# Talking-heads attention and expert layers: two sets' mixes and two score units in one stretch of 64x64 tiles every fourth step, copies out of PSUM dealt to ScalarE and VectorE

## The chip, the core and the metric

The kernel runs on one core of one Trainium2 chip. The metric is the device time of one execution in microseconds (us); three executions of the kernel before took 1455.02, 1460.07 and 1455.32 us, median 1455.32. The engines are TensorE (PE in the profile, with its weight loads as PEld), VectorE (DVE), ScalarE (ACT), GpSimd (POOL) and SyncE (SP), whose queue issues the DMA transfers. Each engine works through its own list of instructions in order.

## The reference

Eight batches, 12 heads, 448 positions, 64 values per head. Scores are mixed over the heads before the softmax (w_pre) and the softmax's result is mixed over the heads after it (w_post); then come the values, and three matrix layers on the 3584 tokens:

```python
scores = scale * np.matmul(q, k.transpose(0, 1, 3, 2))
scores = np.einsum('bhij,hg->bgij', scores, w_pre)
scores = scores - np.max(scores, axis=-1, keepdims=True)
attn = np.exp(scores)
attn = attn / (np.sum(attn, axis=-1, keepdims=True) + 1e-09)
attn = np.einsum('bhij,hg->bgij', attn, w_post)
x = np.matmul(attn, v)
a = x @ w1
b = x @ w2
out = (a * b @ w3) @ w_out
```

## The kernel before

**Attention.** A *score unit* (`qk`, line 173) makes the scores of a pair of heads for 128 rows of queries, four matmuls in 64x64 tiles into two PSUM banks; two copies (lines 178 and 179) bring them to SBUF as `st`, and SyncE stores them to DRAM as `raw`. They are read back as `r` by *sets*: a set is 2 x 10 query rows with all 12 heads, so that heads lie along the partitions. There are 180 sets. For each set `mix` (line 219) multiplies by w_pre (four matmuls in 64x64 tiles into `psm`), `largest` (line 226, VectorE) finds the row minimum of the negated scores (`mn`), `exp` (line 234, ScalarE) makes `e` and its sums `sm`, and `scale` makes the reciprocal `ri` (lines 243 and 244, VectorE) and from it the scaled w_post, `w` (line 246, GpSimd; `w2` in the code). `post` (line 259) multiplies `e` by it: 28 small matmuls in 64x64 tiles into `pso`, which `put` (line 273) copies to `mt` on ScalarE. When `mt` holds 150 columns (15 units of 10), `av` (line 300) multiplies it by the values: 24 matmuls for half of the heads, in 128x64 tiles, into `psa`.

**Background.** Between these, TensorE makes *background matmuls* on the whole 128x128 array, handed out by `advance`: first the fold of two weight matrices (line 359), then the expert layers of batches 0 and 1 (lines 521 and 552), then those of the other batches in pairs by a seven-product scheme (line 701). Each of these groups ends in a *gather* (lines 655 and 657), and each product's inputs are prepared on VectorE (line 620) and *split* into a rounded part `eh` (ScalarE, line 639) and the rest `el` (GpSimd, line 640). In the first 110 steps weights are also *converted* from 64-bit words: four VectorE operations for each piece (lines 116 to 120), a ScalarE square (106), and a split (125, 126). Between steps 107 and 180 VectorE makes sums of weights (lines 462 and 475).

**Order.** The program is in the order in which the code runs; no scheduler moves anything. `run` counts steps n, two for each set (m = n // 2), 366 in all. In an even step `largest` and `exp` of set m run; in an odd step `scale` of set m, then, after the background matmuls, `av` where due, `post` of set m - 1, `mix` of set m + 1, and a score unit. So each set has one stretch of small tiles on TensorE (`pso`, `psm`, `psq`) between two runs of background matmuls. `shares` spreads the background matmuls over the steps so that steps are about equally long. Copies out of PSUM are put on a list (`ends`, and `soon` for what follows them) and issued a little later, by `do_ends` and `do_soon`; transfers are issued at the next step's start (`do_later`). `bank` names one of eight PSUM banks; `psm` has banks 2 and 3, `pso` 4 and 5, `psa` 0, `psq` 0 and 1, the background 6 and 7.

Of the kernel before, what the change touches and what calls it, by code (L numbers as in the profile page):

```python
# [6 lines left out]
F32 = mybir.dt.float32  # L7
# [42 lines left out]
class Kernel:  # L50
# [36 lines left out]
    def bank(self, i, name):  # L87
        if any(b == i for b, _ in self.ends + self.soon):
            self.do_ends()
            self.do_soon()  # L90
        return self.ps.tile([128, 512], F32, tag=f"b{i}", name=name)
# [73 lines left out]
    def qk(self, b, p, c, banks):  # L165
# [13 lines left out]
        (nc.vector.tensor_copy if b == c == 0 else nc.scalar.copy)(st[:, 1], ps[1])  # L179
# [33 lines left out]
    def mix(self, m):  # L213
        nc, r = self.nc, self.rs.pop(m)
        ps = [self.bank(2 + s, f"psm{m}_{s}") for s in range(2)]
# [33 lines left out]
    def post(self, m):  # L249
        nc, w2s = self.nc, self.w2s.pop(m)  # L250
        if any(b in (4, 5) for b, _ in self.ends):
            self.do_ends()
        for s, e in enumerate(self.es.pop(m)[0]):
            for j in range(JB):
                a, z = divmod(j, 2) if j < JB - 1 else (NJ - 1, s)
                at = (2 * a + s) * HK
                for c in range(2):
                    k = slice(c * PP, c * PP + HK)
                    nc.tensor.matmul(self.pso[c][z * PP:(z + 1) * PP, at:at + HK], e[k, j * PP:(j + 1) * PP], w2s[k, s],  # L259
                                     start=True, stop=True)  # L260
        for c in range(2):
            n = 2 * m + c
            w, (b, t) = self.width(n), divmod(n, NB)
# [3 lines left out]
            src = self.pso[c][:, :NJ * 2 * HK].rearrange("p (j s g i) -> p j s g i", j=NJ, s=2, g=H)  # L267
            dst = self.mt[b, a][:, :, :, u * IB:u * IB + w]
            self.ends.append((4 + c, lambda dst=dst, src=src, w=w: self.put(dst, src, w)))

    def put(self, dst, src, w):
        if w == IB:
            self.nc.scalar.copy(dst.rearrange("p j g (s i) -> p j s g i", s=2), src)  # L273
        else:
            for s, k in ((0, IH), (1, w - IH)):
                self.nc.scalar.copy(dst[:, :, :, s * IH:s * IH + k], src[:, :, s, :, :k])
# [3 lines left out]
    def load_v(self):  # L280
# [3 lines left out]
        t = self.vp.tile([128, NJ, 128], F32, tag=f"v{g}", name=f"v{b}_{g}")  # L284
# [6 lines left out]
    def av(self, b, a, g):  # L291
        nc, cols = self.nc, self.cols(a)
        W = cols.stop - cols.start
        if g % 3 == 0:
            self.psa = self.bank(0, f"psa{b}_{a}_{g}")[:, :3 * GB * IB].rearrange("p (g i) -> p g i", g=3)
        v, mt = self.vs[b, g], self.mt[b, a]
        for j in range(NJ):
            for s in range(2):
                rows = slice(s * D, (s + 1) * D)
                nc.tensor.matmul(self.psa[rows, g % 3, :W], v[:, j, rows], mt[:, j, 2 * g + s, :W],  # L300
                                 start=(j == 0), stop=(j == NJ - 1))
        if g % 3 == 2 and b >= ONE:
            q, dst = self.psa[:, :, :W], self.x_d[b][g // 3][:, :, cols]
            x = self.xq.tile([128, 3, GB * IB], F32, tag="x", name=f"xd{b}_{a}_{g}")[:, :, :W]

# [4 lines left out]
            def store():  # L310
                nc.sync.dma_start(dst, x)
                self.x_made[b] += 1

            self.ends.append((0, leave))
        elif g % 3 == 2:
            if b not in self.xs:
                pool = self.xp[b % 2]
                self.xs[b] = [pool.tile([128, K1, S], F32R, tag=f"x{t}", name=f"x{t}{b}") for t in "hl"]
            h, l = (x[:, g - 2:g + 1, cols] for x in self.xs[b])
            q = self.psa[:, :, :W]  # L320
            self.ends.append((0, lambda: nc.scalar.copy(h, q)))
            self.soon.append((0, lambda: nc.vector.tensor_tensor(l, q, h.bitcast(F32), op=ALU.subtract)))
        if a == NG - 1:
            self.later.append(self.load_v)
# [726 lines left out]
```

## Time and profile before

| | us |
|---|---|
| median of three executions | 1455.32 |
| the profiled execution | 1456.61 |
| its span, first to last instruction | 1454.8 |
| TensorE matmuls busy | 1390.1 |
| VectorE busy | 739.0 |
| ScalarE busy | 833.1 |
| GpSimd busy | 620.7 |

A span is the time from the first to the last instruction on the core; the execution's own time is 1.8 us longer. In the view of groups a row gives line, engine, operation, written and read tiles, shape and count, then busy time in us, mean length of one in ns, and idle time of the engine just before with what ended it. In the timeline a row gives start and length in us. In the view of windows a row gives the stretch, the busy time of PE, PEld, DVE, ACT and POOL in it with their instructions, the granted clock of TensorE as a share of full speed, the busy share of the DMA engines and GB/s. One fp32 matmul of 64x64 or 128x64 tiles leaves two records on TensorE, one of the background leaves one.

### The profile page before, as it was taken

How to read it: one execution, taken by the hardware profiler on the slowest of the kernel's cores; microseconds unless marked ns; L12 is line 12 of the kernel's file. 1: busy time of each engine (PE TensorE's matmuls, PEld its weight loads, DVE VectorE, ACT ScalarE, POOL GpSimd, SP SyncE). 2: the span in 40 equal slices, each digit the busy share in tenths (PEclk: the TensorE clock that was granted, in tenths of full speed). 3: DMA queues.
4: the chain of work that ended last, by engine and by line, in shares of the span. 5: the costliest groups of instructions: out<-in, count | busy, mean ns of one | idle time of the engine just before them, and what ended most of it. 6: DMA issues, size and time to landing. Idle time of an engine off the chain costs nothing.

```text
span 1454.8 us, 45722 instructions
## 1 busy us (share of the span) xinstructions
PE 1390.1 (96%) x18684; PEld 1059.4 (73%) x18684; DVE 739.0 (51%) x1497; ACT 833.1 (57%) x1952; POOL 620.7 (43%) x754
## 2 busy tenths in 40 slices
PE   5789998999999989999999999999999999999998
PEld 2357785776677667776777777777776777899988
DVE  4867565767644544432344445334444447334563
ACT  3876665777756656665555656656655546422231
POOL 1333232444324434632244445444335446446683
PEclk7989998999999999999999999999999999999999
DMA  8998789999999999999989988799879766698875
GB/s 256 365 319 274 237 267 287 311 336 307 316 288 353 348 343 319 368 338 314 311 266 291 319 278 280 234 312 350 288 230 285 236 179 214 206 332 263 240 229 173
DMA packets 203760, 416.86 MB, mean 287 GB/s; under 512 B 20528, under 2 KB 120112, under 8 KB 203472
## 3 DMA queue, kind: packets, MB, share of 16 engines
q1 hardware_dynamic: 203552, 413.94, 87.2%
q8 instruction: 149, 2.44, 0.7%
q14 instruction: 59, 0.48, 0.1%
HBM read 279.77 MB, written 134.09 MB: 284 GB/s over the span
## 4 chain that ended last, share of the span: by engine, by line
PE 78%; DMA 13%; DVE 5%; ACT 3%; issue 1%; SPq 0%; POOL 0%; DVEq 0%; ACTq 0%; POOLq 0%
PE e L701 20%; PE psa L300 10%; PE pso L259 10%; PE psm L219 8%; PE psq L173 7%; PE psf L359 5%; PE eg L521 4%; PE e2o L701 4%; PE e1o L701 4%; PE e3o L701 4%; DMA s_d<-s 3%; PE eo L552 3%; DMA cs<-wo 3%; DMA r<-raw_d 2%; DMA wu<-w_d 2%; ACT e L234 1%
## 5 line engine op out<-in xcount | busy, mean ns | idle before, releaser
L246 POOL TENSOR_SCALAR w<-wpo,ri 128x60 f32<-128x60 f32 x360 | 180.7, 518 | 489.0 <-DVE ri L244 465.8
L226 DVE TENSOR_REDUCE mn<-psm 128x1 f32<-128x448 f32 x360 | 207.8, 619 | 317.0 <-PE psm L219 316.6
L701 PE MATMUL e<-eh,wu 128*128 128x448 f32 x1008 | 297.3, 372 | 6.3 <-DVE c L655 3.2
L273 ACT COPY mt<-pso 128x480 f32<-128x480 f32 x352 | 197.8, 621 | 177.3 <-PE pso L259 177.1
L234 ACT ACTIVATE e<-psm,mn 128x448 f32<-128x448 f32 x360 | 226.6, 642 | 9.6 <-DVE mn L226 9.6
L219 PE MATMUL psm<-r,wsc 60*64 60x448 f32 (+1 forms) x1440 | 197.9, 557 | 32.1 <-ACT e L234 19.9
L701 PEld LDWEIGHTS e<-eh,wu 128*128 128x128 f32 x1008 | 188.0, 188 | 52.5 <-issue 27.4
L259 PEld LDWEIGHTS pso<-w,e 60*64 60x64 f32 x10080 | 174.5, 134 | 50.0 <-issue 44.0
L259 PE MATMUL pso<-w,e 60*64 60x60 f32 x10080 | 198.6, 224 | 0.1
L701 PE MATMUL e<-el,wu 128*128 128x448 f32 x504 | 187.1, 371 | 0.0
L173 PE MATMUL psq<-kq 64*64 64x448 f32 x1176 | 159.5, 546 | 0.6 <-ACT st L178 0.6
L300 PE MATMUL psa<-mt,v 128*64 128x150 f32 (+1 forms) x2304 | 156.9, 293 | 1.9 <-ACT st L178 1.9
L300 PEld LDWEIGHTS psa<-mt,v 128*64 128x64 f32 x2304 | 143.6, 137 | 17.9 <-issue 6.3
L655 DVE TENSOR_TENSOR c<-c,e 128x448 f32<-128x448 f32 x168 | 101.8, 618 | 87.6 <-PE e L701 82.8
L178 ACT COPY st<-psq 128x448 f32<-128x448 f32 x162 | 86.4, 533 | 68.8 <-ACT mt L273 32.8
L521 PE MATMUL eg<-xh,wu 128*128 128x448 f32 x384 | 118.8, 380 | 4.8 <-DMA wu<-w_d 4.8
L640 POOL TENSOR_TENSOR el<-x,eh 128x448 fp32r<-128x448 f32 x90 | 104.2, 1176 | 34.8 <-ACT eh L639 34.8
L701 PEld LDWEIGHTS e<-el,wu 128*128 128x128 f32 x504 | 94.9, 188 | 22.4 <-issue 14.1
L243 DVE TENSOR_SCALAR sa<-sm 128x2 f32<-128x2 f32 x180 | 35.9, 200 | 129.6 <-ACT e L234 129.0
L173 PEld LDWEIGHTS psq<-kq 64*64 64x64 f32 x1176 | 62.2, 136 | 53.8 <-issue 29.8
L521 PEld LDWEIGHTS eg<-xh,wu 128*128 128x128 f32 x384 | 71.8, 190 | 38.1 <-issue 25.3
L179 ACT COPY st<-psq 128x448 f32<-128x448 f32 x162 | 87.7, 541 | 0.0
(99 smaller groups left out, 2011.5 us busy)
## 6 DMA issues: line engine op xcount, KB each, us to landing
r<-raw_d SPq DMA_DIRECT2D x344, 210.0 KB, 4.9
raw_d<-st SPq DMA_DIRECT2D x138, 448.0 KB, 5.4
wu<-w_d SPq DMA_DIRECT2D x104, 384.0 KB, 6.4
wu<-s_d SPq DMA_DIRECT2D x96, 384.0 KB, 4.8
wu<-w_d SPq DMA_DIRECT2D x51, 512.0 KB, 5.6
kq<-kq SPq DMA_DIRECT2D x42, 448.0 KB, 6.2
wu<-s_d SPq DMA_DIRECT2D x36, 512.0 KB, 4.9
x<-x_d SPq DMA_DIRECT2D x72, 224.0 KB, 6.3
```

Source lines behind the costliest of these rows:

```text
L173: nc.tensor.matmul(ps[s][z * PP:(z + 1) * PP], t[rows, q:q + PP], t[rows, k:k + S], start=True, stop=True)
L219: nc.tensor.matmul(ps[s][c * PP:(c + 1) * PP, :S], self.wsc[k], r[k, c], start=True, stop=True)
L226: self.nc.vector.tensor_reduce(mn[:, s:s + 1], self.psm[m][s][:, :S], axis=AX.X, op=ALU.min)
L234: nc.scalar.activation(e, p[:, :S], AF.Exp, bias=mn[:, s:s + 1], scale=-1.0, accum_out=sm[:, s:s + 1])
L246: nc.gpsimd.tensor_scalar_mul(w2[:, s], self.wpo, ri[:, s:s + 1])
L259: nc.tensor.matmul(self.pso[c][z * PP:(z + 1) * PP, at:at + HK], e[k, j * PP:(j + 1) * PP], w2s[k, s], start=True, stop=True)
L273: self.nc.scalar.copy(dst.rearrange("p j g (s i) -> p j s g i", s=2), src)
L300: nc.tensor.matmul(self.psa[rows, g % 3, :W], v[:, j, rows], mt[:, j, 2 * g + s, :W], start=(j == 0), stop=(j == NJ - 1))
L521: nc.tensor.matmul(p, u[:, k % (K1 // 2), x], xs[y][:, k], start=(k == 0 and t == 0), stop=(k == K1 - 1 and t == 2))
L640: nc.gpsimd.tensor_tensor(lo, x, hi.bitcast(F32), op=ALU.subtract)
L655: nc.vector.tensor_tensor(a[out], a[to[0]], p, op=ALU.add)
L701: nc.tensor.matmul(p, w[:, k, x], ops[m, k][y], start=(k == 0 and t == 0), stop=(k == nk - 1 and t == 2))
```

## The change

Steps now come in cycles of four, for two sets m and m + 1. Steps 0 and 1 run `largest` and `exp` of one set each, step 2 runs `scale` of both, and step 3 runs, after `av` where due, `post` of both, one score unit, `mix` of the next two sets, and the other score units, all in one stretch. `do_soon` stands before `largest` and `scale` in each step; the conversions and sums (`convert`) follow them, and in step 3 stand at its end. `psm` and `pso` of a set share two banks, 4 and 5 or 0 and 1, that are never given back (`fixed`); `psa` and all score units use banks 2 and 3. The second `st` copy and the second `put` copy run on VectorE. `put` always copies all 480 columns; since a bank now holds old scores in columns that `post` doesn't write, the last 64 rows of the values are padded with zeros in two versions, and `av` multiplies the last values in two halves of 75 columns: 30 matmuls instead of 24. `shares` weighs the steps by new numbers, and the steps of score units and `av` are dealt anew.

```diff
@@ qk
-        (nc.vector.tensor_copy if b == c == 0 else nc.scalar.copy)(st[:, 1], ps[1])
+        nc.vector.tensor_copy(st[:, 1], ps[1])
@@ mix
-        ps = [self.bank(2 + s, f"psm{m}_{s}") for s in range(2)]
+        ps = [self.bank((4, 0)[m % 2] + s, f"psm{m}_{s}") for s in range(2)]
@@ post
+        ps = [self.bank((4, 0)[m % 2] + c, f"pso{m}_{c}") for c in range(2)]
...
-            self.ends.append((4 + c, lambda dst=dst, src=src, w=w: self.put(dst, src, w)))
+            copy = nc.vector.tensor_copy if c else nc.scalar.copy
+            self.ends.append(((4, 0)[m % 2] + c, lambda copy=copy, dst=dst, src=src: copy(dst, src)))
@@ av
+            for j in range(NJ - 1):
+                for s in range(2):
+                    rows = slice(s * D, (s + 1) * D)
+                    nc.tensor.matmul(ps[rows, g], self.vs[b, u][:, j, rows], mt[:, j, 2 * u + s], start=(j == 0), stop=False)
+            for t in range(2):
+                for s in range(2):
+                    rows = slice(s * D, (s + 1) * D)
+                    out, x = (y.rearrange("p (u z i) -> p u z i", z=2, i=IH)[:, :, t] for y in (ps[rows, g], mt[:, NJ - 1, 2 * u + s]))
+                    nc.tensor.matmul(out, self.vs[b, u][:, NJ - 1 + t, rows], x, start=False, stop=(t == 1))
@@ run
-            if m < SETS:
-                if odd:
-                    self.scale(m)
-                else:
-                    self.largest(m)
             self.do_soon()
...
+            if at < 2 and m + at < SETS:
+                self.largest(m + at)
+            elif at == 2 and m < SETS:
+                self.scale(m)
+                self.scale(m + 1)
+            if at < 3:
+                convert()
             advance(now // 2)
             self.do_ends()
-            if not odd and m < SETS:
-                self.exp(m)
+            if at < 2 and m + at < SETS:
+                self.exp(m + at)
             advance(now - now // 2)
             for x in avs.get(n, []):
                 self.av(*x)
+                self.do_ends()
...
-            if odd and 1 <= m <= SETS:
-                self.post(m - 1)
-            if odd and m + 1 < SETS:
-                self.mix(m + 1)
-            self.do_ends()
-            for i, x in enumerate(qks.get(n, [])):
-                self.later.append(self.qk(*x, (6, 7) if i else (0, 1)))
+            if at == 3 and m < SETS:
+                for x in (m, m + 1):
+                    self.post(x)
+                    self.do_ends()
+                scores()
+                for x in (m + 2, m + 3):
+                    if x < SETS:
+                        self.mix(x)
+            while units:
+                scores()
+            self.do_ends()
+            if at == 3:
+                self.do_soon()
+                convert()
```

On TensorE, in the pair stage, the list around the post of sets 118 and 119 (`w2118` and `e118` are w and e of set 118, `r120` the scores of set 120, `e11_...` the background) read before, with "..." for rows that only repeat:

```order
L701 MATMUL e11_7_3_0_12635<-el11_7_1_12458,wu130_12446 128x448
L259 MATMUL pso0_141<-w2118_12550,e118_0_12530 64x60
...
L219 MATMUL psm120_0_12690<-r120_12513,wsc_138 64x448
...
L173 MATMUL psq6_2_2_0_12698<-kq6_2_12092 64x448
...
L701 MATMUL e11_7_3_0_12635<-eh11_7_1_12457,wu130_12446 128x448
```

In this piece one set's post, the mix of the set after the next, and a score unit stand between two background matmuls; set 119 has its own such piece later. Of the change, on TensorE, the end of the same place:

```order
L258 MATMUL bank1_142<-w2119_12569,e119_1_12542 64x60
L173 MATMUL psq6_2_1_0_12656<-kq6_2_12053 64x448
...
L219 MATMUL bank4_143<-r120_12482,wsc_138 64x448
...
L219 MATMUL bank0_141<-r121_12485,wsc_138 64x448
...
L173 MATMUL psq6_2_2_0_12673<-kq6_2_12053 64x448
...
L696 MATMUL e11_7_3_1_12587<-eh11_7_0_12290,wu131_12361 128x448
```

Both posts (118 and 119, of which the last row is shown), two score units and both mixes now stand in one piece, and the mix of sets 118 and 119 stood in the piece just before it.

GpSimd at the same sets, before (`el11_5_0` is one of three rests that a product needs):

```order
L246 TENSOR_SCALAR w2118_12550<-wpo_140,ri118_12549 128x60 x2
L640 TENSOR_TENSOR el11_5_0_12556<-x11_12_0_11682,eh11_5_0_12555 128x448
L246 TENSOR_SCALAR w2119_12646<-wpo_140,ri119_12645 128x60 x2
L640 TENSOR_TENSOR el11_5_1_12652<-x11_12_1_11683,eh11_5_1_12651 128x448
L640 TENSOR_TENSOR el11_5_2_12656<-x11_12_2_11684,eh11_5_2_12655 128x448
```

and of the change:

```order
L635 TENSOR_TENSOR el11_5_0_12525<-x11_12_0_11649,eh11_5_0_12524 128x448
L635 TENSOR_TENSOR el11_5_1_12553<-x11_12_1_11650,eh11_5_1_12552 128x448
L635 TENSOR_TENSOR el11_5_2_12557<-x11_12_2_11651,eh11_5_2_12556 128x448
L246 TENSOR_SCALAR w2118_12562<-wpo_140,ri118_12561 128x60 x2
L246 TENSOR_SCALAR w2119_12569<-wpo_140,ri119_12568 128x60 x2
```

The three rests, which stood behind the weights w of set 118, now stand ahead of those of both sets.

VectorE in the stage of conversions, at sets 28 and 29 (`ca45` and `cx45` are conversion 45, `mn28` the minima of set 28), before:

```order
L120 SCALAR_TENSOR_TENSOR cx45_3379<-cm45_3373,ca45_3375 128x384
L226 TENSOR_REDUCE mn28_3435<-psm28_0_3410 128x1
L226 TENSOR_REDUCE mn28_3435<-psm28_1_3411 128x1
L243 TENSOR_SCALAR sa28_3456<-sm28_3446 128x2
L244 RECIPROCAL ri28_3457<-sa28_3456 128x2
```

and of the change:

```order
L179 COPY st2_2_0_3419<-psq2_2_0_1_3414 128x448
L116 TENSOR_SCALAR ca45_3426<-cs45_3266 128x384
...
L226 TENSOR_REDUCE mn28_3445<-bank4_143 128x1
...
L226 TENSOR_REDUCE mn29_3465<-bank0_141 128x1
...
L116 TENSOR_SCALAR ca46_3472<-cs46_3315 128x384
...
L120 SCALAR_TENSOR_TENSOR cx46_3476<-cm46_3470,ca46_3472 128x384
L243 TENSOR_SCALAR sa28_3494<-sm28_3451 128x2
```

Conversion 45 now stands between the last score copy and the minima of set 28, and the minima of set 29 and conversion 46 between those and the sums of set 28.

143 lines of the change are left out of this document (68 added, 75 removed).

## Prediction

> **What bounds the kernel now.** I read the page first: busy shares, then the chain that ended last by engine.
>
> ```profile
> span 1454.8 us, 45722 instructions
> PE 1390.1 (96%) x18684; PEld 1059.4 (73%) x18684; DVE 739.0 (51%) x1497; ACT 833.1 (57%) x1952; POOL 620.7 (43%) x754
> PE 78%; DMA 13%; DVE 5%; ACT 3%; issue 1%; SPq 0%; POOL 0%; DVEq 0%; ACTq 0%; POOLq 0%
> ```
>
> TensorE is the bound: 64.7 us of the span are all that it is not busy. So the change can win only by what TensorE does between useful columns, and can lose by whatever makes it wait, however idle that engine is on average. Next the timeline of one set in the pair stage, all engines (start, length, engine, line).
>
> ```profile
> 742.24 0.67 PE L701 MATMUL e<-eh,wu 128*128 128x448 f32 x2
> 742.34 0.53 ACT L178 COPY st<-psq 128x448 f32<-128x448 f32 x1 [0.38 <-PE psq L173]
> 742.75 0.62 DVE L655 TENSOR_TENSOR c<-c,e 128x448 f32<-128x448 f32 x1
> 743.19 0.65 ACT L234 ACTIVATE e<-psm,mn 128x448 f32<-128x448 f32 x1
> ...
> 744.33 0.22 ACT L234 ACTIVATION_READ_ACCUMULATOR e<-psm,mn 128x1 f32 x1
> 744.42 1.52 ACT L639 CAST eh<-x 128x448 fp32r<-128x448 f32 x3
> ...
> 745.11 0.16 DVE L243 TENSOR_SCALAR sa<-sm 128x2 f32<-128x2 f32 x1
> 745.37 0.17 DVE L244 RECIPROCAL ri<-sa 128x2 f32<-128x2 f32 x1
> 745.39 0.56 PE L701 MATMUL e<-eh,wu 128*128 128x448 f32 x2
> 745.71 0.84 POOL L246 TENSOR_SCALAR w<-wpo,ri 128x60 f32<-128x60 f32 x2 [5.53 <-DVE ri L244]
> 745.79 0.37 PE L701 MATMUL e<-el,wu 128*128 128x448 f32 x1
> 746.09 1.08 PE L259 MATMUL pso<-w,e 60*64 60x60 f32 x55
> 746.50 3.34 POOL L640 TENSOR_TENSOR el<-x,eh 128x448 fp32r<-128x448 f32 x3
> ...
> 746.95 0.98 PE L219 MATMUL psm<-r,wsc 60*64 60x448 f32 x7
> 747.70 0.98 PE L173 MATMUL psq<-kq 64*64 64x448 f32 x8
> 747.96 1.16 DVE L226 TENSOR_REDUCE mn<-psm 128x1 f32<-128x448 f32 x2 [2.42 <-PE psm L219]
> 748.61 0.67 PE L701 MATMUL e<-eh,wu 128*128 128x448 f32 x2
> ```
>
> See two things. First, TensorE runs 18 background matmuls in 3.85 us (742.24 to 746.09) and the stretch in 64x64 tiles in 2.52 us (to 748.61) without a hole. Second, the softmax weights w, whose set was mixed just before 742, are done at 746.55, but this stretch's post used the set before; these weights are first used in the next stretch, 6 us later. That slack is why no small engine is on the path.
>
> **The change, part by part.**
>
> *Fewer stretches.* By the program orders TensorE returns from small tiles to background matmuls 185 times before and 101 times after: 84 fewer. The price of one is in the rows above. Background matmuls follow each other by 0.20 us (745.39 to 745.79 for two), the last before the stretch takes 0.30: 0.10. The eight psq at the end take 0.91 where the eight psm of the same width take 0.75: 0.16. The first pair after it lasts 0.67 instead of 0.56: 0.11. Together 0.36 us; I drop four stretches of the load-bound start: 80 x 0.36 = **-29 us**. Switches between attention times values (64 columns) and 64x64 tiles stay near 45 on both sides.
>
> *Values in 30 instead of 24 matmuls.*
>
> ```profile
> 758.04 3.28 PE L300 MATMUL psa<-mt,v 128*64 128x150 f32 x48
> 761.25 1.08 PE L259 MATMUL pso<-w,e 60*64 60x60 f32 x55
> ```
>
> The trace counts two records per matmul. 48 records take 3.21 us, 67 ns each, on two tiles: 134 ns per tile for 150 columns. In pso 56 take 0.86 us (to 746.95 above), on four tiles: 61 ns for 60 columns. The line through both gives 73 ns for 75 columns, 36.5 per record. Per eight batches 576 records of 67 ns become 1152 of 36.5: +3.4, and 150 columns instead of 148 in a third of them +0.7: **+4 us**. Bounds: 0 if halves cost half, +39 if each costs 67. I stay by the line, since both its rows are this mode's neighbours.
>
> ```profile
> L701 PEld LDWEIGHTS e<-eh,wu 128*128 128x128 f32 x1008 | 188.0, 188 | 52.5 <-issue 27.4 <-DVE c L655 5.6 <-DVE mn L226 2.1
> ```
>
> The upper end is what a rule would make of it. In the Trainium skill, page "TensorE: Matmul & The Clock Gate", section Part 3, The mechanism, weight loads overlap running matmuls only when the row groups differ; values use all 128 rows in both tiles, so each added matmul would show its load bare. By that the sum would be up to 35 us worse than by the line. The row speaks against it: loads of 188 ns on all 128 rows fit between matmuls 200 ns apart.
>
> *Waits that go.* TensorE's waits, 95 to 670 us and 670 to 1300:
>
> ```profile
> PE psm L219 <- ACT e L234: 12.2, 9, 5.8
> PE psm L219 <- ACT e L234: 0.7, 1, 0.7
> 234.91 8.63 DMA cs<-w
> ```
>
> The next mix waits for the exp that frees its bank; banks are dealt anew, so this goes, except the 5.8, which sits behind the load in the chain's row: **-7 us**.
>
> *The wait that comes.* Before, post follows its mix by two stretches; now by one. TensorE is in order, so everything stands behind a late post. I count from the first background matmul after a stretch. Until post TensorE has n x 0.214 us (18 in 3.85): 21 matmuls a cycle in the conversion stage (sets 26 to 53) 4.5 us; 27 in the next (54 to 91) 5.8; 35 in the pair stage (92 to 179) 7.5. Where values stand first (40 of 90 cycles) add 3.3.
>
> Against it stands the shortest chain, now that the last st copy is VectorE's (0.62, by the row below, ends at 0.7): two pairs of reductions 2.32, sa and ri 0.43, hop 0.17, w 0.84, hop 0.1: 4.6 us. That alone fits. What the orders put into it:
>
> ```profile
> L179 DVE COPY sz<-psq 128x448 f32<-128x448 f32 x6 | 3.6, 620 | 0.3
> 321.89 0.35 DVE L116 TENSOR_SCALAR ca<-cs 128x384 int32<-128x384 int32 x1
> 323.56 0.56 DVE L120 SCALAR_TENSOR_TENSOR cx<-cm,ca 128x384 f32<-128x384 f32 x1
> L475 DVE TENSOR_TENSOR y<-y 128x768 f32<-128x768 f32 (+3 forms) x33 | 29.5, 893 | 0.1
> L462 DVE TENSOR_TENSOR y<-wu 128x384 f32<-128x384 f32 (+1 forms) x44 | 25.2, 587 | 2.6 <-DMA wu<-w_d 2.4 <-DMA s_d<-s 0.2
> ```
>
> - Conversion stage: a conversion is four VectorE operations in 2.23 us (321.89 to 324.12). With two in the chain, as in the order of sets 28 and 29, w is there at 9.1, a wait of 4.6. Cycles without values: 28, 34, 44 wait 4.5 each, 26 (14 matmuls) 6; 36, 42 and 50 have one conversion and wait about 1.3. With values 32, 38, 40 and 46 wait 1. Sum **+27**.
> - Next stage: sums of mean 0.72 us (33 of 893 ns, 44 of 587). 58 has five in the chain (8.2 against 5.8), 64, 74 and 82 four (7.5); 80 has a GpSimd part: 2.4 + 3 x 1.7 + 1.2 = **+9**.
> - Pair stage: here do_soon now stands ahead of scale, so parts el (1.11 us, 3.34 for three), whose casts eh (0.51) stand behind the second exp on ScalarE, come ahead of w on GpSimd. In the rows above w (745.71) went ahead of them. Exp of the second set (1.36, 743.19 to 744.55) waits for its reductions, which stand behind a gather of 0.62 that waits for TensorE; it ends at 4.8 to 5.3. Cast, two parts, w and hops: 4.8 + 0.56 + 2.27 + 0.94 = 8.6 to 9.1 against 7.5; on average 1.2. One part: 0.3; three, at 94 with 27 matmuls, 3.5. Of 23 cycles without values 3 have no part there, 6 one, 13 two, one three: 1.8 + 15.6 + 3.5 = **+21**.
> - Sets 0 to 25: three or four conversions a cycle, but loads set the pace and 47 to 51 background matmuls cover later. By the chain 0 to 13; I take **+6**.
>
> *The clock.*
>
> ```profile
> 1117.17 0.44 PE L701 MATMUL e<-eh,wu 128*128 128x448 f32 x1 [2.41 <-DMA wu<-w_d]
> 1115.00:1120.00 5.00, 2.83 (x66) 1.82 (x66) 0.00 (x0) 1.12 (x3) 3.29 (x4) 0.82 1.02 280
> 1120.00:1125.00 5.00, 5.00 (x23) 4.01 (x20) 3.06 (x7) 2.99 (x8) 2.19 (x3) 0.84 0.68 204
> ```
>
> A hole of 2.41 us cost granted clock: (0.18 + 0.16) x 5 = 1.7 us of full speed. Holes that long now come in 26, 28, 34, 44 and 94: **+8 us**; others sit at the edge, so 0 to 14.
>
> *Evictions.* VectorE gains 180 put copies of 0.66 (0.62 x 480/448) and 162 st copies of 0.62, 219 us, and stands near 960 of 1495; ScalarE loses about 200. As busy time that bounds nothing; as a queue it is the chain above.
>
> *Transfers.*
>
> ```profile
> r<-raw_d SPq DMA_DIRECT2D x344, 210.0 KB, 4.9
> 400.00:530.00 130.00, 127.97 (x1974) 94.78 (x1974) 60.90 (x127) 81.80 (x193) 54.27 (x63) 1.00 0.99 331
> ```
>
> The scores r of two sets are now asked for together on SyncE, three steps ahead of their mixes instead of three of each: some 8 us, against 4.9 to landing, with the stores and loads of kq of the same step queued behind. Loads of values grow by a quarter, 3.1 of 416.86 MB. From 400 to 530 us the DMA engines are 0.99 busy, so a late r can show: 0 to 5 us, and I take nothing, since a slower TensorE asks for less per us.
>
> Sum: -29 + 4 - 7 + 27 + 9 + 21 + 6 + 8 = +39 us. The profiled execution took 1456.6 us, 1.8 around its span; the median is 1.3 lower. So 1456.6 + 39 - 1.3 = **1494 us**.
>
> **The rivals.**
>
> *Faster: the waits stay hidden.* Only stretches, values and old waits count: -32, so 1423 us. It decides at post: if w is done before 4.5, 5.8 and 7.5 us, TensorE sees nothing. For it: 40 cycles are covered by values, and GpSimd is idle for 57% of the span. Against: the orders put conversions and parts into the chain, and a queue in order cannot pass them. The skill's page "TensorEngine Tiling (Array Packing)", section PSUM Bottleneck, advises both ScalarE and VectorE for emptying PSUM, which by itself would speak for this rival; the waits of before show no matmul that waited for a put.
>
> *Half the waits.* If exps and conversions mostly run before I place them, 63 becomes about 30 and no hole costs clock: 1453 to 1465 us.
>
> *Heavier.* Holes of 1.2 to 2.4 us also lower the clock, which lengthens post and mix, which start the next chain late: 1520 to 1540. Values at 67 ns per record would end there too: 1494 + 35 = 1529.
>
> *It doesn't merge.* The orders show 67 stretches of two posts, psq, two mixes, psq. It merges; no chance kept.
>
> **How the numbers follow.** Forecast (1475 to 1520) 0.53, half the waits (1440 to 1475) 0.20, hidden 0.14, heavier 0.13 (0.05 of it the values). The range leaves out the hidden case and the end of the heavier: 1446 to 1535. Half a per cent, about what a measurement of this kernel can tell, is 7 us: faster 0.14 + 0.03, same 0.08, slower 0.75.
>
> **What would show it.** TensorE's waits of pso on POOL w: near 60 us in all, longest 4 to 6 us in the conversion stage, none where psa stands ahead. Stretches near 100, each 0.36 us of switching. 60 psa records in about 3.3 us. Granted clock dips around sets 26 to 45. I am wrong if pso hardly waits, or if psm waits for put copies instead.

## The result, and the profile after

| | before | after |
|---|---|---|
| median of four executions, us | 1455.17 | 1600.69 |
| lowest to highest, us | 1450.36 to 1460.07 | 1594.78 to 1602.39 |
| granted clock of TensorE over the span | 0.985 | 0.949 |

The changed kernel takes 1.0993 times as long (95% interval 1.0946 to 1.1039): 145.5 us slower, where 39 were forecast. The profiled execution took 1599.89 us. The head of the page after, with busy times by engine and the chain that ended last:

```profile
span 1598.1 us, 47077 instructions
PE 1418.1 (89%) x19260; PEld 1118.0 (70%) x19260; DVE 991.2 (62%) x1839; ACT 690.0 (43%) x1602; POOL 618.3 (39%) x754
PE 57%; DVE 14%; issue 10%; DMA 9%; POOL 6%; ACT 2%; SPq 1%; DVEq 0%; POOLq 0%; ACTq 0%
```

TensorE still has most of the busy time, but idles for 180.0 us of the span instead of 64.7, and VectorE now has 14% of the chain instead of 5%. No engine besides TensorE is busy for more than 62%: what grew is waiting. TensorE's longest waits, after (us in total, times, longest):

```profile
PE bank L258 <- POOL w L246: 76.5, 34, 10.1
PE e L696 <- DVE c L650: 12.4, 14, 2.3
PE psq L173 <- DVE xl L317: 11.0, 7, 2.5
PE psq L173 <- issue: 9.6, 8, 1.5
PE bank L219 <- DMA r<-raw_d: 8.9, 1, 8.9
PE psq L173 <- ACT st L178: 8.4, 7, 2.5
PE bank L258 <- issue: 8.0, 5, 4.0
```

and before, the two rows of the same view that answer to them:

```profile
PE psm L219 <- ACT e L234: 19.9, 15, 5.8
PE e L701 <- DVE c L655: 3.2, 5, 1.5
```

The foretold wait of post on the weights w is there, 76.5 us, or 84.5 with the row put down to issue, which the trace does not tie to w; and the mix's wait on exp is gone as foretold. Rows that the prediction did not have are those behind VectorE: `xl` (the rest of a values product, which holds the bank that the next score unit needs) and the gathers `c`.

One cycle of the conversion stage, sets 34 and 35, from the timeline of after (start, length, engine, line):

```profile
336.41 0.62 DVE L179 COPY st<-psq 128x448 f32<-128x448 f32 x1 [1.63 <-PE psq L173]
...
336.95 0.35 DVE L116 TENSOR_SCALAR ca<-cs 128x384 int32<-128x384 int32 x1
337.33 0.56 DVE L117 SCALAR_TENSOR_TENSOR ca<-cs,ca 128x384 int32<-128x384 int32 x1
337.84 1.01 POOL L126 TENSOR_TENSOR wu<-cx,wu 128x384 fp32r<-128x384 f32 x1 [5.83 <-ACT wu L125]
337.93 1.34 DVE L118 SCALAR_TENSOR_TENSOR ca<-cs,ca 128x384 int32<-128x384 int32 x1
...
339.88 2.21 DVE L226 TENSOR_REDUCE mn<-bank 128x1 f32<-128x448 f32 x4
...
342.00 0.35 DVE L116 TENSOR_SCALAR ca<-cs 128x384 int32<-128x384 int32 x1
...
344.15 0.16 DVE L243 TENSOR_SCALAR sa<-sm 128x2 f32<-128x2 f32 x1
...
344.45 0.99 POOL L126 TENSOR_TENSOR wu<-cx,wu 128x384 fp32r<-128x384 f32 x1 [5.59 <-ACT wu L125]
...
345.42 2.41 POOL L246 TENSOR_SCALAR w<-wpo,ri 128x60 f32<-128x60 f32 x4
...
346.01 3.31 PE L258 MATMUL bank<-w,e 60*64 60x60 f32 x112 [5.17 <-POOL w L246]
```

VectorE works almost without a pause from the copy at 336.41 to the reciprocals: copy, conversion, minima, conversion, scale. GpSimd's weights come last, behind a subtraction of the conversion before (344.45) in GpSimd's own queue, and post starts 5.17 us late. The same stretch by windows (busy time of PE, PEld, DVE, ACT, POOL, then granted clock, DMA share, GB/s):

```profile
335.00:340.80 5.80, 5.80 (x37) 4.22 (x29) 4.19 (x7) 1.67 (x4) 1.01 (x1) 1.00 0.82 227
340.80:343.60 2.80, 0.04 (x1) 0.00 (x0) 2.68 (x6) 2.80 (x10) 0.00 (x0) 1.00 0.99 361
343.60:346.00 2.40, 0.00 (x0) 0.00 (x0) 2.22 (x7) 1.62 (x4) 1.55 (x3) 0.51 0.30 102
346.00:350.50 4.50, 4.49 (x120) 3.63 (x124) 2.69 (x5) 1.24 (x2) 2.80 (x4) 0.50 0.76 251
350.50:356.00 5.50, 5.50 (x39) 4.04 (x32) 4.85 (x10) 3.95 (x11) 0.27 (x1) 1.00 0.54 149
```

The hole starts at 340.84. From 343.6 the granted clock is 0.5, and it stays there until 350.5: all of the late post runs at half speed. So the hole is paid for twice, and the second payment is nearly half of the first.

**Where the 145 us stand.** Added up from the matmul rows of the two traces: TensorE's idle time grew by 115 us; its busy time in stretches at half clock grew from 38 to 133 us, of which half is lost (+47); its work itself, counted at full speed, shrank by 19. The sum is 143, the difference of the spans. (The clock's rows begin some 9 us into the span; the 5 us of work before them ran at half speed by their spacing, and are counted so on both sides.)

### The profile page after: what moved, and what is told of

It reads as the page before. It is cut to its first block, busy times and chain, and to the rows that moved or that the text cites. A ratio compares the mean times of both kernels' runs of the same rounds, so it can differ in the third digit from the quotient of the medians.

```text
span 1598.1 us, 47077 instructions
## 1 busy us (share of the span) xinstructions
PE 1418.1 (89%) x19260; PEld 1118.0 (70%) x19260; DVE 991.2 (62%) x1839; ACT 690.0 (43%) x1602; POOL 618.3 (39%) x754
## 4 chain that ended last, share of the span: by engine, by line
PE 57%; DVE 14%; issue 10%; DMA 9%; POOL 6%; ACT 2%; SPq 1%; DVEq 0%; POOLq 0%; ACTq 0%
PE e L696 12%; PE bank L258 10%; PE bank L219 8%; PE psq L173 7%; PE psa L291 6%; DVE mn L226 3%; PE e3o L696 3%; PE psf L354 2%; PE eo L547 2%; DMA wu<-w_d 2%; POOL w L246 2%; DMA r<-raw_d 2%; PE psa L296 2%; DVE ca L118 2%; PE e2o L696 2%
## 5 line engine op out<-in xcount | busy, mean ns | idle before, releaser
L234 ACT ACTIVATE e<-bank,mn 128x448 f32<-128x448 f32 x360 | 225.2, 633 | 120.2 <-DVE mn L226 115.9
L258 PE MATMUL bank<-w,e 60*64 60x60 f32 x10080 | 196.0, 234 | 84.8 <-POOL w L246 76.5
L258 PEld LDWEIGHTS bank<-w,e 60*64 60x64 f32 x10080 | 181.1, 146 | 109.5 <-POOL w L246 95.2
L268 DVE COPY mt<-bank 128x480 f32<-128x480 f32 x180 | 117.9, 657 | 212.7 <-PE bank L258 212.4
L226 DVE TENSOR_REDUCE mn<-bank 128x1 f32<-128x448 f32 x360 | 204.9, 617 | 8.7 <-PE bank L219 8.7
L179 DVE COPY st<-psq 128x448 f32<-128x448 f32 x162 | 101.1, 624 | 170.7 <-PE psq L173 153.0
L219 PE MATMUL bank<-r,wsc 60*64 60x448 f32 (+1 forms) x1440 | 177.2, 571 | 16.5 <-DMA r<-raw_d 8.9
L268 ACT COPY mt<-bank 128x480 f32<-128x480 f32 x180 | 111.9, 624 | 180.9 <-PE bank L258 180.8
L178 ACT COPY st<-psq 128x448 f32<-128x448 f32 x162 | 86.3, 533 | 186.5 <-PE psq L173 174.5
L291 PE MATMUL psa<-mt,v 128*64 128x150 f32 x1728 | 140.8, 299 | 11.0 <-ACT st L178 6.0
L650 DVE TENSOR_TENSOR c<-c,e 128x448 f32<-128x448 f32 x168 | 101.1, 615 | 60.8 <-PE e L696 55.5
L516 PEld LDWEIGHTS eg<-xh,wu 128*128 128x128 f32 x384 | 74.0, 194 | 33.5 <-issue 14.2
```

Of the source, the lines that this page charges most:

```text
L179: nc.vector.tensor_copy(st[:, 1], ps[1])
L219: nc.tensor.matmul(ps[s][c * PP:(c + 1) * PP, :S], self.wsc[k], r[k, c], start=True, stop=True)
L226: self.nc.vector.tensor_reduce(mn[:, s:s + 1], self.psm[m][s][:, :S], axis=AX.X, op=ALU.min)
L234: nc.scalar.activation(e, p[:, :S], AF.Exp, bias=mn[:, s:s + 1], scale=-1.0, accum_out=sm[:, s:s + 1])
L258: nc.tensor.matmul(ps[c][z * PP:(z + 1) * PP, at:at + HK], e[k, j * PP:(j + 1) * PP], w2s[k, s], start=True, stop=True)
L268: self.ends.append(((4, 0)[m % 2] + c, lambda copy=copy, dst=dst, src=src: copy(dst, src)))
```

## The experiments

Each edit is against the changed kernel unless it says otherwise. Theory one, at first: post waits for w, and the holes cost clock. Its rival: the merged order, or the copies on VectorE, cost by themselves.

**Without the late weights.** `post` multiplies by the constant w_post, so it waits for no w; the division by the sums is left out of the result.

```diff
-    nc.tensor.matmul(ps[c][...], e[k, j * PP:(j + 1) * PP], w2s[k, s], start=True, stop=True)
+    nc.tensor.matmul(ps[c][...], e[k, j * PP:(j + 1) * PP], self.wpo[k], start=True, stop=True)
```

> Post multiplies by the unscaled w_post, so it waits for no GpSimd result; scale and its GpSimd work still run. This leaves out the softmax's normalisation. Theory (posts wait for late w, 84 us in the changed kernel's trace, and the holes lower the clock, 47 us): the waits go, and some 30 us of the clock's loss with them; posts then wait at most for the second set's e. 1601 - 84 - 30 = about 1485 us (1465 to 1515), half-clock time near 60 us instead of 133. Rival (the merged stretch or the copies on VectorE are slow, and the wait for w is only where it shows): another wait takes its place and the time stays above 1560 us.

Measured 1559.85 us (ratio to before 1.0721, interval 1.0686 to 1.0757): 41 us less, not the 85 or more expected. TensorE's waits in it:

```profile
PE psq L173 <- DVE xl L317: 17.8, 7, 4.6
PE bank L258 <- ACT e L234: 12.5, 20, 2.7
```

The wait on w is gone, and others have grown. The late weights are a part of the loss, and not all of it.

**Minima and scale ahead of the parts.** `do_soon` behind `largest` and `scale`, as it stood before.

```diff
-            self.do_soon()
...
             elif at == 2 and m < SETS:
                 self.scale(m)
                 self.scale(m + 1)
+            self.do_soon()
```

> largest and scale stand ahead of do_soon again, as before the change, so parts el no longer stand ahead of w on GpSimd. Theory: the pair stage loses most of its 15.8 us of waits for w and half of its 17 us at half clock; the conversion stage keeps its 40 us. 1570 to 1590 us. Rival (in the pair stage w is late because of VectorE's queue, not GpSimd's): the pair stage's waits stay above 12 us and the time moves by less than 5 us.

Measured 1579.53 us (1.0849, 1.0810 to 1.0889). The pair stage alone by windows, after and then this run:

```profile
777.10:1408.50 631.40, 592.82 (x8874) 473.95 (x8875) 390.16 (x713) 288.19 (x671) 269.25 (x339) 0.99 0.79 260
```

```profile
774.20:1387.50 613.30, 589.98 (x8874) 469.24 (x8875) 354.45 (x713) 288.60 (x671) 268.11 (x338) 1.00 0.81 268
```

18 of the 21 us come from there, and in the two windows post's wait on w falls from 14.2 to 0.5 us. In this stage `do_soon` issues casts on ScalarE and work on GpSimd, and nothing on VectorE, so it is GpSimd's queue that held w. The prediction's term for the parts ahead of w (+21 in the pair stage) is confirmed in place, and nearly in size.

**Filling the holes.** 162 matmuls without use, into a spare bank, ahead of eleven posts of the conversion stage, so that TensorE is busy where it waited for w.

```diff
+                for i in range({26: 27, 28: 23, 32: 7, 34: 23, 36: 8, 38: 7, 40: 13, 42: 9, 44: 23, 46: 13, 50: 9}.get(m, 0)):
+                    ...
+                    nc.tensor.matmul(spare[:, :S], fill[:, :128], fill[:, 128:128 + S], start=True, stop=True)
                 for x in (m, m + 1):
                     self.post(x)
```

> In the conversion stage the holes ahead of eleven posts are filled with 162 matmuls of 0.204 us on weights at hand, into a spare bank that nobody reads; nothing else changes, and no wait gets shorter. Theory (holes lower the clock by themselves): the 41.6 us that TensorE works at half clock between sets 24 and 54 fall below 15, and the time falls by 10 to 20 us, to 1581 to 1591. Rival (the clock falls for another reason, as the mean load): half-clock time stays above 30 us there and the time is 1600 us or more, since any surplus matmul adds.

Measured 1575.62 us (1.0836, 1.0795 to 1.0877). The conversion stage by windows, after and with the filler:

```profile
264.10:500.90 236.80, 187.24 (x2883) 139.49 (x2883) 165.43 (x318) 108.71 (x262) 74.55 (x103) 0.89 0.77 248
```

```profile
265.90:492.50 226.60, 206.70 (x3041) 163.44 (x3041) 165.47 (x318) 108.79 (x262) 74.89 (x103) 0.98 0.80 259
```

The granted clock goes from 0.89 to 0.98 and the stage is 10 us shorter, though no input of post came earlier by the edit. So the clock is lost to the holes and is a cost of its own. The other 15 us of the median, which comes out under the expected 1581 to 1591, are not explained: they lie partly in later stages, where nothing was edited, and are not claimed for it.

**Everything of the softmax early.** Minima and exponentials of both sets at the start of step 0, scale at its end, conversions behind.

```diff
+            if at == 0 and m < SETS:
+                self.largest(m)
+                self.largest(m + 1)
+            self.do_soon()
+            if at:
+                convert()
...
+            if at == 0:
+                if m < SETS:
+                    self.scale(m)
+                    self.scale(m + 1)
+                convert()
```

> The merged stretch and all copies stay, but the chain is issued earlier: largest and exp of both sets at the start of step 0 ahead of do_soon, scale of both at its end, the conversions behind it, and that of step 3 ahead of the posts. Theory: w is ready 4.6 to 6 us after the stretch in all stages, so the waits for w fall from 84 to under 15 us and the clock's loss under 20: 1440 to 1480 us, perhaps below the kernel before if only stretches and values count (1423). Rival (the merge itself costs, in the small tiles or in copies): above 1520 us.

Measured 1591.90 us (1.0957, 1.0909 to 1.1006): a miss. Post hardly waits for w any more, but the mix waits 26.8 us for put copies on ScalarE and 11.0 for those on VectorE, and the score units 19.6 for `xl`. By the order, what makes those late is the work pushed behind the softmax. So late weights cannot be the whole cause, and the second theory is that VectorE's queue, with 220 us of copies in it, sets the pace of the loop.

**All copies back on ScalarE.**

```diff
-        nc.vector.tensor_copy(st[:, 1], ps[1])
+        (nc.vector.tensor_copy if b == c == 0 else nc.scalar.copy)(st[:, 1], ps[1])
...
-            copy = nc.vector.tensor_copy if c else nc.scalar.copy
+            copy = nc.scalar.copy
```

> The changed kernel with every copy of scores and mixed values back on ScalarE, in the changed order (some 220 us of copies leave VectorE's queue and stand in ScalarE's, which had 690 us). Theory A (VectorE's queue, lengthened by the copies, is what TensorE waits for): post's wait on w in the conversion stage falls from 40 us to 15-30, the waits on xl and on the second set's put shrink, and the time is 1540-1575. Theory B (the merged order itself is the cost, wherever the copies run): within 10 us of the changed kernel, 1590-1610, with the waits as they were. Theory C (ScalarE becomes the bound, since exponentials stand behind the copies): over 1610, with post waiting for e instead of w.

Measured 1546.93 us (1.0632, 1.0613 to 1.0650): 54 us less, by the edit that takes work from the engine that is busy for 62% and gives it to the other. Its page and first wait:

```profile
PE 1412.9 (91%) x19260; PEld 1121.6 (73%) x19260; DVE 778.7 (50%) x1497; ACT 827.6 (54%) x1944; POOL 625.3 (40%) x754
```

```profile
PE bank L258 <- POOL w L246: 51.5, 30, 9.3
```

The wait on w falls by 25 us, and the score units' wait on `xl` (11.0) leaves the list: theory A, and not the rival that the merged order alone costs.

**The copies dealt in the old order.** Against the kernel before:

```diff
-        (nc.vector.tensor_copy if b == c == 0 else nc.scalar.copy)(st[:, 1], ps[1])
+        nc.vector.tensor_copy(st[:, 1], ps[1])
...
+            copy = nc.vector.tensor_copy if c else nc.scalar.copy
+            self.ends.append((4 + c, lambda dst=dst, src=src, w=w, copy=copy: self.put(dst, src, w, copy)))
...
```

> The kernel before, in its own order, with the copy of the second mixed bank and of the second score bank on VectorE. Theory A: VectorE's queue with these copies in it makes TensorE wait in the order of before too, 1470-1500, with post waiting for w or mix for VectorE's copy. Theory B (dealing costs nothing; only the merged order does): 1450-1460.

Measured 1486.34 us (1.0213, 1.0192 to 1.0234): +31. Dealing them costs there too, and TensorE has waits behind VectorE that the kernel before did not have, or had at 3.2 us (`c`):

```profile
PE psq L173 <- DVE st L179: 7.5, 7, 1.7
PE psq L173 <- DVE xl L323: 7.5, 11, 0.9
PE pso L259 <- DVE mt L274: 7.2, 7, 1.8
PE e L702 <- DVE c L656: 5.5, 8, 1.5
```

A rival is that the copies slow other work down by running beside it, on VectorE or on GpSimd. The traces leave little room for it: in the conversion stage the four operations of a conversion (L116 to L120) take 79.1 us in all after the change and 74.3 with the copies on ScalarE, and w takes 0.53 and 0.54 us a piece.

**Both repairs, normalisation left out.** Constant weights in `post` and all copies on ScalarE, the two diffs above together.

> The changed kernel with the mixed values multiplied by the constant weights (the normalisation by the sum is left out of the product, so post waits for no w) and with every copy on ScalarE. Theory A: both reasons are gone, and what is left over the kernel before is small, 1470-1520, under the 1560 of the plain weights alone. Theory B (the merged order is the cost): about that 1560, 1545-1570. Theory C (ScalarE's queue is as bad a place): over 1570.

Measured 1511.97 us (1.0399, 1.0366 to 1.0431). The conversion stage of the kernel before, of the copies on ScalarE, and of both repairs:

```profile
229.20:419.20 190.00, 180.28 (x2847) 127.91 (x2845) 122.75 (x259) 134.90 (x322) 73.65 (x102) 0.97 0.95 313
```

```profile
247.90:452.90 205.00, 179.34 (x2883) 136.37 (x2883) 126.14 (x261) 134.01 (x320) 75.75 (x103) 0.95 0.87 286
```

```profile
243.10:433.50 190.40, 176.49 (x2883) 129.64 (x2879) 127.55 (x267) 133.52 (x322) 76.70 (x104) 0.98 0.95 315
```

236.8 us, then 205.0, then 190.4 against 190.0 before: in this stage the two causes account for the whole loss. Over the kernel they give 89 of 145 us, nearly the sum of what each gives alone (41 + 54). 57 us are left, in other stages.

**One kind of copy on VectorE.** Constant weights, score copies on ScalarE, second puts on VectorE.

> Plain weights (the normalisation is left out of the product), score copies on ScalarE, second puts still on VectorE (118 us there): between the run with both on VectorE (1560) and with neither (1512). Theory A (the loss goes with the time added to VectorE's queue, 118 of some 230 us): 1530-1540. Theory B (puts shared by two engines free the mix's bank sooner, the score copies do the harm): under 1515. Theory C (the puts alone do it): 1550-1560.

Measured 1528.32 us (1.0505, 1.0469 to 1.0541), between 1512 (none) and 1560 (both). The two kinds as groups on the page after the change (busy time, mean ns):

```profile
L268 DVE COPY mt<-bank 128x480 f32<-128x480 f32 x180 | 117.9, 657 | 212.7 <-PE bank L258 212.4
L179 DVE COPY st<-psq 128x448 f32<-128x448 f32 x162 | 101.1, 624 | 170.7 <-PE psq L173 153.0
```

The puts, 117.9 us of busy time, cost 16; the score copies, 101.1 us, another 32. Both kinds cost. The time lies just under the range that goes by their busy time alone, by less than its interval can tell.

**The early order with all copies on ScalarE, and with the puts on VectorE.** The diff of the early order with both lines of the copies, or with the score line alone.

> The changed kernel with both sets' minima, exponentials and scales at the start of the cycle, ahead of conversions and parts (as in the run before that moved them early and came to 1592), and now with every copy on ScalarE. Theory A (the early order missed because VectorE's queue, with the copies in it, kept other products late: parts xl, gathers, puts): 1505-1525, as much as the run with plain weights and all copies on ScalarE (1512). Theory B (early minima only move the wait, whoever copies): 1535-1550, no better than the copies alone (1547). Theory C (ScalarE now has early exponentials and all copies in one queue, and becomes the wait): over 1550.

> The same early order, with the score copies on ScalarE and only the second put of each set on VectorE (118 us of copies there instead of about 230). Theory A (time grows with what stands in VectorE's queue): between the two ends, 1540-1570. Theory B (the score copies, which end a stretch, did the harm; puts on VectorE free the mix's bank sooner): under 1525, below the run with all copies on ScalarE. Theory C (the puts did it): 1580-1600.

Measured 1550.68 us (1.0668, 1.0640 to 1.0696) and 1583.54 us (1.0894, 1.0862 to 1.0925). The first is a miss for theory A: no better than the copies alone (1546.93). Its first waits:

```profile
PE bank L219 <- ACT mt L268: 29.3, 13, 6.6
PE psq L173 <- DVE xl L317: 15.0, 7, 4.4
```

With the softmax first, the conversions land in the last steps of the cycle, ahead of puts and `xl`. The time stands on the border of theories B and C, and the first wait, on ScalarE's puts, is what C names, though it was 26.8 us with the copies dealt, too. In each order tried here one of the conversions, the softmax and the copies is late; the order picks which. The second came out as its theory C had it: in the early order the puts on VectorE alone take back 33 of the 41 us that both kinds cost there (1591.90 against 1550.68), more than their 16 in the run above. So which copy costs most depends on the order.

**Both repairs with the computation whole.** Minima and scale ahead of the parts, and all copies on ScalarE.

> The whole computation in the merged order, with the minima and scales ahead of the parts (alone 21 us under the changed kernel) and every copy on ScalarE (alone 54 us under it). Theory A (the two act on different stages: the first on the pair stage, the second on the conversion stage and the start): they add up, 1520-1535. Theory B (both take away the same wait): 1540-1550.

Measured 1526.19 us (1.0492, 1.0465 to 1.0519): 1600.7 - 21 - 54 = 1526. They add up. It is the fastest whole version of the merged order here, and still 71 us behind the kernel before. Its posts still wait 36.4 us for w; none of the runs points to a version that beats the kernel before.

**The price of the values alone.** Against the kernel before: padded values, 30 matmuls instead of 24.

```diff
-        for j in range(NJ):
+        for j in range(NJ - 1):
...
+        for t in range(2):
+            for s in range(2):
+                ...
+                nc.tensor.matmul(out, v[:, NJ - 1 + t, rows], x, start=False, stop=(t == 1))
```

> The kernel before with the last values padded and the product with the values in 30 instead of 24 matmuls, nothing else changed. The prediction's term: +4 (1457-1462), no new wait. Upper bound of the prediction: +39 (1494), every matmul at the rate of a wide one. TensorE's 48 records in 3.2 us become 60 in about 3.3.

Measured 1462.64 us (1.0057, 1.0034 to 1.0081): +7.7, interval +5 to +12. One unit from its timeline:

```profile
763.31 0.99 PE L300 MATMUL psa<-mt,v 128*64 128x150 f32 x12
...
766.23 0.47 PE L305 MATMUL psa<-mt,v 128*64 128x75 f32 x8
```

The 60 records run from 763.31 to 766.70, 3.39 us, where 48 took 3.28: a record of half the width costs a little over half.

**The price of a return to the background.** Against the kernel before, one small matmul in the middle of each even step's background.

```diff
             if not odd and m < SETS:
                 self.exp(m)
+                nc.tensor.matmul(self.pso[0][:HK, 480:512], self.wpo[:HK], self.wpo[:HK, :32], start=True, stop=True)
```

> The kernel before with one small matmul in 64x64 tiles (60 rows, 32 columns, into unused columns of a bank) in the middle of the background matmuls of every even step: up to 180 more returns from small tiles to background matmuls, and nothing else. The prediction's price of a return without the scores' share (0.10 + 0.11 us): +38, 1490-1496. Theory now, from the spacing of the matmuls in the two traces (background matmuls 218.1 to 214.6 ns on average over 2270, for 84 fewer returns: 0.1 us each): +18, 1468-1478.

Measured 1503.05 us (1.0332, 1.0300 to 1.0364), above both ranges. TensorE returns 358 times instead of 185, 173 more: 0.28 us each, with the small matmul itself and the way to it. In TensorE's busy time it is 0.36 us each (1390.1 to 1451.9 us); some of that came back as idle time, which fell from 64.7 to 51.2. The prediction's price was nearer than the later one from mean spacing. At 0.28 us, 84 fewer returns are worth about 24 us, an estimate.

**Work between post and mix.** The first two tries held back background matmuls of the cycle's last step:

```diff
+            hold = 6 if at == 3 and now >= 12 and m + 2 < SETS else 0
...
                 scores()
+                advance(hold)
```

> The early order with all copies on ScalarE, and six background matmuls of the cycle moved into the stretch, between the posts with their scores and the next mixes. Theory A (inside the merged stretch a mix waits for the puts of the bank that a post has just filled, so TensorE needs other work between them): mix's waits on puts go from about 10 us to under 3, and the time is 5-15 below the early order alone, in spite of some 80 more returns of 0.1 us. Theory B (those waits are small and the returns cost): 5-15 above it.

> The run with plain weights and all copies on ScalarE (1512; the normalisation is left out of the product), and six background matmuls of the cycle moved into the stretch, between the posts with their scores and the next mixes. What is left of the loss there is some 57 us against the kernel before. Theory A (a good part is the mix waiting, inside the merged stretch, for the puts of the bank that the post has just filled: mix's records take 116 ns there instead of 101, some 16 us, and its waits on puts and copies 10): 1490-1500 in spite of some 80 returns more. Theory B (the rest is spread over transfers, expert operands and the clock, and the mix's place doesn't matter): 1515-1535, the price of the returns on top.

That step has none to hold back, so nothing moved. The runs, 1553.25 and 1511.32 us, are repeats of 1550.68 and 1511.97 and decide nothing; they show how well such a time repeats. The next one took the six from the step before (`at == 2`):

> As the run before it meant to do and did not (there the cycle's last step has no background matmuls, so nothing moved and the program was that of 1512 again): plain weights (the normalisation is left out of the product), all copies on ScalarE, and now six background matmuls from the cycle's third step held back until behind the posts and their scores, ahead of the mixes, in sets 26 to 177. Some 66 more returns to background matmuls at 0.28 us, as the run with added switches gave, are +18. Theory A (mix waits in the merged stretch for the puts of its own bank, 16 us in lengthened records and 10 in listed waits): -26 + 18, 1500-1510, and mix's records at about 101 ns instead of 111 to 116. Theory B (the rest of the loss lies elsewhere): the returns are paid on top, 1520-1532.

Measured 1527.02 us (1.0491, 1.0456 to 1.0526). From the spacing of the matmul records at full clock, without the idle time of the list of waits: the mix's mean went from 110.8 ns in the run of 1512 to 100.6, as before the change (101.0). So the mix did wait there, and in that run's timeline its weight loads (PEld) wait for a put on ScalarE:

```profile
913.15 0.13 PEld L219 LDWEIGHTS bank<-r,wsc 60*64 60x64 f32 x1 [0.18 <-ACT mt L268]
```

In the changed kernel itself the mean is 99.5 ns, with constant weights alone 104.3 and with the copies on ScalarE alone 106.2, so this wait came with the two repairs. But two rows of the waits show the price, first of 1512 and then of this run:

```profile
PE bank L258 <- ACT e L234: 6.7, 6, 2.5
```

```profile
PE bank L258 <- ACT e L234: 18.0, 22, 3.9
```

The matmuls that now cover the mix are missing where they covered the softmax, and the returns are paid on top. Theory A had the mechanism, theory B the time.

## Why the prediction was wrong, point by point

The direction and the place of the waits on w were right; the size, 39 for 145, was not. Term by term, from the two traces: the clock costs 39 us more than forecast, waits other than on w 38, the wait on w 21, and TensorE's own work 6; that is 104, the span's growth of 143 less the 39.

- **Fewer stretches, -29.** The measured price of 0.28 us makes -24 of 84 fewer. In the traces TensorE's work, counted at full speed, shrank by 19 with the added values in it, where -25 was forecast for both. About right.
- **Values, +4.** The run of its own gave +7.7 (+5 to +12). The mechanism was right, since the line through the two rows holds; the size was a few us too low.
- **Waits that go, -7.** The mix's wait on exp (19.9 us with the start of the kernel) left the list. This was right; waits of the mix for puts came in its place (4.4 us after the change, 8.3 in the run of 1512, and the longer records there).
- **The wait that comes, +63.** The list has 84.5 us with the row of issue. The cycles with two conversions were foretold well: 28, 34 and 44 wait 5.2 each (4.5 foretold) and 26 waits 6.0 (6); so was the pair stage, 15.8 (21). The others were too low: 36, 42 and 50 wait 2.1 to 2.3 (1.3), and 32, 38, 40 and 46, which values should have covered, 1.7 to 3.0 (1), so that the conversion stage has 38.1 for 27; the next stage has 13.5 for 9, and sets 0 to 25 17.0 for 6. Taken away, this wait is worth 41 us and not 84: other waits grow then, as the run with constant weights showed.
- **The clock, +8.** The first step that failed. Five holes of 2.4 us or more were counted; the trace after has 19 such gaps of TensorE where before had 6, and 55 of 1.2 us or more where before had 18. Of the 19, 12 stand at a post (one of them, at 54, put down to issue), and the other 7 are about what the kernel before had. So the long holes came from post, as foretold, but more than twice as many: those of the start (sets 6 and 24), of two cycles with values (40 and 46) and of three others (54, 58 and 124) were put too low or at nothing. By the half-clock time above the clock cost +47. The change has 27 stretches of half clock where before had 7: 47 for 20 more is 2.4 us each, where 1.7 was taken. The larger error was their number.
- **Evictions, 0.** The step that failed most, by the experiments: "As busy time that bounds nothing; as a queue it is the chain above". In the chain above stood one copy of 0.62 us, ahead of the minima. But all that VectorE makes stands in that queue: conversions, sums, gathers, `xl`, and every one of these holds a bank or an operand of TensorE. With the copies taken off it the kernel is 54 us faster in the new order, and with them put on it 31 slower in the old. (The 54 us overlap with the two terms above: 25 of them are wait on w.) By the list of waits, waits other than on w grew by some 30 us where the forecast had them shrink by 7. In the Trainium skill, page "TensorEngine Tiling (Array Packing)", section PSUM Bottleneck, the advice is to use both engines for emptying PSUM; these runs differ, by 54 and 31 us: here VectorE had other work in its queue that TensorE waits for.
- **Transfers, 0.** Mixes waited 8.9 us for r, and 11.1 before. This was right.
- **The rivals.** "Heavier" (1520 to 1540, holes that lower the clock and lengthen post) was the nearest, and its mechanism, the clock, came; it was held too small and given 0.13, and no rival had the copies in VectorE's queue. The signs of being wrong that were named (post hardly waits, or the mix waits for puts instead) did not come, since they looked at w and the mix alone.

What stays open: with both causes away and the price of the values taken off, some 50 us are left in spite of the 24 saved, so about 73 are lost to something else. In that run TensorE idles 36 us more than before and loses 20 more to the clock, and the mix's records hold 14 more; behind these stand ten or so small waits (`st`, puts, `xl`, gathers, expert weights), most of 2 to 10 us in all. They come with the merged order, but no single one was shown to carry them, and putting work between post and mix did not win them back. Two things that came with the merged order were not tested apart from it: that `psm` and `pso` of a set share their banks, and all score units and the values banks 2 and 3. Whether a longer distance between mix and post (a cycle more, with more banks) would win them back was not tried.

## What to carry to other kernels

An engine's idle share does not tell what a job costs in its queue: ask what stands behind the job, and which TensorE operand or bank that product holds. Where one consumer in order waits for many small products, count the slack of each of them before shortening a loop, and not that of the product which looks nearest. And price a hole at about one and a half times its length, if the clock answers to it as it did here (115 us more of idle time, and 47 lost to the clock).

## What the runs showed of the hardware

- How long a hole must be to cost clock. In the trace after, from 50 us on, 16 of the 17 holes of 2.4 us or more have a stretch of half clock that begins in them or within 7 us behind; of the 10 between 1.8 and 2.4 us it is 6, of the 25 between 1.2 and 1.8 us 3. (In each of these two groups one hole shares its stretch with another hole.) Such a stretch lasts mostly 3.4 or 6.8 us (343.6 to 350.5 above) and so falls on the work that was late already.
- VectorE's conversion operation of 0.56 us took 1.34 beside a GpSimd subtraction on SBUF (337.84 and 337.93 above), and GpSimd's four w took 2.41 us beside VectorE's conversions, where the prediction's row has two in 0.84. Over the trace after, that operation (L118, 384 columns) lasts 0.56 us in all 32 cases without GpSimd work beside it, and 0.93 on average in the 32 with such work. Its minima and its put copies, which read PSUM alone, do not show this: they last 0.62 and 0.66 us with and without. This was seen in rows and not tested by itself.
